# mLSTM attention with a bilinear layer on one core: a gate table for the first time chunk, later gates moved, a longer search for the order, and tiles on multiples of 128 bytes

## The chip, the core and the metric

The kernel runs on one core of one Trainium2 chip. The metric is the device time in microseconds (us) of one execution, the median of several runs. The engines of the core are named as in the profile: PE (TensorE, the matmuls), PEld (the loading of its weights), DVE (VectorE), ACT (ScalarE), POOL (GpSimd) and SP (SyncE, which here issues every DMA).

## The reference

Gated linear attention over 4 batches, 8 heads, 768 time steps and 40 columns per head, and behind it a bilinear layer on all 3072 tokens:

```python
for t in range(S):                                   # S = 768, for each of 4 x 8 heads
    m_new = max(f[t] + m, i[t])
    f_stab = exp(f[t] + m - m_new);  i_stab = exp(i[t] - m_new);  m = m_new
    C = f_stab * C + i_stab * outer(v[t], k[t]);  n = f_stab * n + i_stab * k[t]
    y[t] = sigmoid(o[t]) * (C @ q[t]) / max(abs(n . q[t]), 1)
x = y as (3072 tokens, 8 * 40 = 320)
out = ((x @ w_a) * (x @ w_b)) @ w_out                # 320 -> 1536 -> 320
```

The three weights are float64; the other inputs are float32.

## The kernel before

**Attention.** Time is cut into 6 chunks c of 128 steps, so there are 24 pairs n = (c, b) of a chunk and a batch. Inside a pair the recurrence becomes matrix products under a mask, with tables of gate terms; between chunks of one batch the state `cst` is carried. `first_gates` makes the running maximum and sums of the gates for chunk 0, `later_gates` for chunks 1 to 5: scans and sums on DVE over tiles of 32 rows (32 = batch times head), which lie in `qks2` and `qks3`. From them come `g_dram` (sent out by a DMA and read back, spread over 128 rows, as `gbc`), and `gtab`, a table with time on the partitions, made by transposes on PE (`ptg`) and an Exp on ACT. The pairs below NS = 2 are done ahead of everything else; the pairs 2 to 5 (`early_chunk`, with `begin_a`, `begin_b`, ...) use plain float32 matmuls, the later ones bf16 pieces.

**The bilinear layer.** Its token blocks have 2, 2, 3, 3, 3, 3, 3, 2 and 3 pairs of 128 tokens (`sizes`). For each block and each of 12 slices `ff` of 128 hidden columns, `up` makes two sums `pu` of 8 float32r matmuls each (x and the weights are each split into a high and a low part, `xh`, `xl` and the two planes of `w`), DVE multiplies them to `g`, this is split into `gh` and `gl`, and `down`, two slices later, adds 3 matmuls per token tile to `pd`. So a block makes 12 * (16 + 3 * tiles) such matmuls.

**Conversion of the weights.** The weights arrive as 32 slices `raw0` to `raw31` of float64 bits. Each passes through `high` (ACT), `low` (DVE for the first five, ACT after), `join` (DVE, the operation on `cw`), `lead_part` (a copy into `w` by ACT or DVE) and `low_part` (a DVE subtraction into `w`). Block 0 uses the slices as they get ready; from block 1 on all are there.

**What sets the order.** The program is first recorded as nodes. A list scheduler, `Plan.run`, then places them with a cost for each (`Plan.cost`), and `settle` repeats this `TURNS` times with disturbed ranks, replays each order under four sets of disturbed costs, and keeps the one with the least mean end. Copies may go to ACT or DVE (`copier`), some sums to DVE or POOL (`adder`): the scheduler chooses. Each engine then runs its instructions in the order written, and waits where its next one isn't ready. While PE would wait in the first part, the scheduler lays in small matmuls `warm` (bf16, 256 columns, result unused); this ends as soon as another tile of the same PSUM buffer `pd2` is used, which `ptg` is.

The attention beside the blocks is one generator, which starts so:

```python
def rest():
    gates = later_gates()
    for _ in range(2):
        next(gates)
        yield
    yield from begin_a(NS)
    yield from begin_e(NS)
    yield from gates
```

All recorded instructions have the profile's line L522, the `warm` matmuls L515 (L528 and L521 in the changed file).

Of the kernel before, what the change touches and what calls it, by code (L numbers as in the profile page):

```python
# [18 lines left out]
AF = mybir.ActivationFunctionType  # L19
ALU = mybir.AluOpType  # L20
PSUM = bass.MemoryType.PSUM
TURNS = 40
TRIALS = 4
SPREAD = 0.3
LANES = 8
# [80 lines left out]


class Node:
    __slots__ = ("i", "eng", "alts", "calls", "by", "prev", "next", "table", "acc", "wide", "use", "pair", "least")

    def __init__(self, i, alts):
        self.i, self.alts, self.eng = i, alts, alts[0]
        self.calls, self.prev, self.next, self.acc = [], {}, [], []
        self.by = {e: [0.0, 0.0, 0.0, False] for e in alts}
        self.table, self.wide, self.use = None, True, 0.0


class Plan:
# [8 lines left out]

    def __init__(self, nc):
        self.nc, self.nodes, self.filler, self.bank = nc, [], None, None
        self.pair, self.least = False, 0.0  # L130
# [50 lines left out]
    def cost(self, node, by, eng, op, out, refs, args, kw):  # L181


        cols = int(np.prod(out.shape[1:]))
        size = [x.size if isinstance(x, View) else mybir.dt.size(x.dtype) for x in refs]
        psum = [isinstance(x, View) and x.root.ring[0] == "psum" for x in refs]
        if eng == "PE":
            if op == "transpose":
                occ = 0.109
            else:  # L190
                f32 = [str(x.dtype) if not isinstance(x, View) else x.kind() for x in refs[1:3]]
                if size[1] == 2:
                    occ = cols / 2400 + 0.005 if cols > 64 else 0.026
                elif "float32r" in f32[0]:
                    occ = cols / 2400 + 0.0135
                else:
                    occ = 0.224 if cols <= 128 else cols / 600 + 0.01
                    if refs[1].shape[0] <= 64:
                        occ = 0.135
                    elif out.shape[0] <= 64:  # L200
                        occ = 0.06
            by[0] += occ
            by[1] = 0.17
            plain = size[1] == 4 and op == "matmul" and "float32r" not in f32[0]
            node.use += cols * refs[1].shape[0] * (1 + plain) / 128.0 * out.shape[0] / 128.0
        elif eng == "ACT":
            func = str(args[2]) if op == "activation" else "Copy"
            node.table = "S" if "Sigmoid" in func else "E" if "Exp" in func else None
            bias = hasattr(kw.get("bias"), "shape")
            by[0] = 0.04 + cols * (0.00084 if any(psum) else 0.00094) + (0.13 if bias else 0.0)  # L210
            by[0] += 0.05 if "Prelu" in func or "scale" in kw else 0.0
            by[1] = 0.11
        elif eng == "DVE":
            rate = 960.0
            one = op in ("tensor_copy", "copy", "tensor_scalar", "memset", "tensor_scalar_max") and not any(psum)
            if one:
                rate = 1920.0 if max(size) == 4 else 3840.0
            if op == "tensor_tensor_scan":
                rate = 480.0
            by[0] = 0.065 + cols / rate  # L220
            by[1] = 0.085
            by[3] = (one or len(refs) > 2) and not any(psum)
        elif eng == "POOL":
            by[0] = 0.03 + cols * 0.00205
            if op == "affine_select":
                by[0] = 0.05 + cols * 0.001
            elif op == "memset":
                by[0] = 0.05 + cols * 0.0008
            by[1] = 0.06
            by[3] = op != "memset"  # L230
        elif op == "dma_start_transpose":
            by[0], by[1] = 1.3, 1.6
        else:
            n = int(np.prod(out.shape)) * size[0]
            node.wide = out.shape[-1] * size[0] > 512
            by[0], by[1] = 0.47 if node.wide else 0.6, 1.7
            by[2] = n / (305e3 if node.wide else 160e3)

    def link(self):
        last, rings = {}, {}  # L240
        for node in self.nodes:
            for key, box, write in node.acc:
                if isinstance(key, Root):
                    if key.first is None:
                        key.first = node
                        rings.setdefault(key.ring, []).append(key)
                    else:
                        self.edge(key.first, node, order=True)
                    key.users.append(node)
                mine = last.setdefault(key, [])  # L250
                for k, b, w in mine:
                    if (w or write) and k is not node and all(p < y and x < q for (p, q), (x, y) in zip(b, box)):
                        self.edge(k, node)
                if write:
                    mine[:] = [
                        z for z in mine
                        if not all(x <= p and q <= y for (p, q), (x, y) in zip(z[1], box))
                    ]
                mine.append((node, box, write))
        for ring in rings.values():  # L260
            for a, b in zip(ring, ring[1:]):
                self.edge(a.first, b.first, order=True)
            for a, b in zip(ring, ring[ring[0].ring[2]:]):
                for k in a.users:
                    self.edge(k, b.first)
# [18 lines left out]
    def run(self, rank, forward=True, fixed=None, odds=None):  # L284
# [18 lines left out]
        order, count, filling = [], 0, False  # L303

        def put(x, r):
            if forward:
# [51 lines left out]
        while count < len(nodes):  # L358
# [56 lines left out]
            if e == "PE" and forward:  # L415
# [6 lines left out]
                while filling and fixed is None:  # L422
# [130 lines left out]
def kernel(  # L553
# [77 lines left out]
    nc.gpsimd.affine_select(  # L631
        mask, mask, pattern=[[1, P]], compare_op=ALU.is_ge, fill=-1e30, base=0, channel_multiplier=-1
    )
    one = wpool.tile([BH, 1], F32, name="one")
    nc.gpsimd.memset(one, 1.0)

    plan.least = 2.1
# [96 lines left out]
    def first_gates():  # L734
# [11 lines left out]
        for j in range(3):  # L746
            x = gb3[j]
            (nc.scalar.copy if j < 2 else nc.vector.tensor_copy)(stk[j * BH:(j + 1) * BH], top(x))
            if j < 2:
                nc.vector.tensor_tensor(gb3[j + 1], x, top(x), op=ALU.subtract)  # L750

    def later_gates():
        f, i, m = (x[:, P:] for x in (gf, gi, gm))
        G = tab[0:BH]
# [3 lines left out]
        nc.vector.tensor_tensor(f, f, m, op=ALU.subtract)  # L758
        nc.vector.tensor_tensor(i, i, m, op=ALU.subtract)
        yield  # L760
        nc.scalar.copy(G[:, 0], gb3[0][:, 0])
        nc.scalar.copy(tab[BH:2 * BH, 0], gb3[0][:, 1])
        for c in range(1, NC):
            nc.vector.tensor_tensor_scan(
                G[:, c], one.broadcast_to([BH, P]), gf[:, c * P:(c + 1) * P], 0.0,
# [1 line left out]
            )  # L767
            if c == 3:
                yield
        nc.sync.dma_start(g_dram.rearrange("c g t -> g c t"), G)  # L770
        ends = wpool.tile([BH, NC - 2, BH // 2], F32, name="ends")
        nc.gpsimd.tensor_tensor(
            ends, G[:, 1:NC - 1, P - 1:].broadcast_to([BH, NC - 2, BH // 2]),
# [4 lines left out]
        nc.vector.tensor_tensor(tab[BH:2 * BH, 1:], beta, G[:, 1:], op=ALU.subtract)  # L778
        yield
        nc.vector.tensor_tensor(  # L780
            tab[2 * BH:], tab[BH:2 * BH], G[:, :, P - 1:P].broadcast_to([BH, NC, P]), op=ALU.add
        )
        yield
        for half in range(2):
            pt = ps_dn.tile([P, 512], F32, tag="pd2", name="ptg")
            n3 = NC // 2
            for c in range(n3):
                nc.tensor.transpose(
                    pt[:, c * 3 * BH:(c + 1) * 3 * BH], tab[:, half * n3 + c, :],
                    ident[0:3 * BH, 0:3 * BH],  # L790
                )
            n0, n1 = (BH, n3 * 3 * BH) if half == 0 else (0, (n3 * 3 - 1) * BH)
            nc.vector.tensor_copy(
                gtab[:, half * (n3 * 3 - 1) * BH:][:, 0:n1 - n0], pt[:, n0:n1]
            )
            yield
        x = gtab[:, BH:].rearrange("p (c g) -> p c g", g=3 * BH)[:, :, 0:2 * BH]
        nc.scalar.activation(x, x, AF.Exp)
        pt = ps_dn.tile([P, 512], F32, tag="pd2", name="pdec")[:, 0:(NC - 2) * BH // 2]
        nc.tensor.matmul(  # L800
# [3 lines left out]
        nc.scalar.activation(dec.rearrange("p c x -> p (c x)"), pt, AF.Exp)  # L804
        yield

    def g_col(c, b, x):
        return gtab[:, (3 * c + x) * BH + b * H:][:, 0:H]

    def beta_col(c, b):  # L810
        return g_col(c, b, 0)
# [1 line left out]
    def w_col(c, b):  # L813
        return g_col(c, b, 1)

    def a_col(c, b):
        return g_col(c - 1, b, 2)


    def weight_stages():  # L820
# [778 lines left out]
```

## Time and profile before

| | |
|---|---|
| median of 3 runs | 534.51 us (534.0 to 534.91) |
| profiled execution | 534.12 us, its span 532.3 us, mean granted TensorE clock 0.994 |
| DVE busy | 411.4 us (77%), 919 instructions |
| ACT busy | 236.3 us (44%), 568 instructions |
| POOL busy | 147.9 us (28%), 194 instructions |

A span runs from the first to the last instruction of the profile; 1.8 us of the execution lie around it. In rows of the timeline stand the start, the busy time, the engine, line and operation, the tiles as output <- inputs with their shape, how many like instructions the row joins, and in brackets how long the engine had been idle before it and what ended that. Rows of groups give the count, then total busy us and mean ns of one. PE's matmuls are pipelined, so what one costs is read from start to start.

### The profile page before, as it was taken

How to read it: one execution, taken by the hardware profiler on the slowest of the kernel's cores; microseconds unless marked ns; L12 is line 12 of the kernel's file. 1: busy time of each engine (PE TensorE's matmuls, PEld its weight loads, DVE VectorE, ACT ScalarE, POOL GpSimd, SP SyncE). 2: the span in 40 equal slices, each digit the busy share in tenths (PEclk: the TensorE clock that was granted, in tenths of full speed). 3: DMA queues.
4: the chain of work that ended last, by engine and by line, in shares of the span. 5: the costliest groups of instructions: out<-in, count | busy, mean ns of one | idle time of the engine just before them, and what ended most of it. 6: DMA issues, size and time to landing. Idle time of an engine off the chain costs nothing.

```text
span 532.3 us, 12505 instructions
## 1 busy us (share of the span) xinstructions
PE 523.2 (98%) x4862; PEld 497.1 (93%) x4862; DVE 411.4 (77%) x919; ACT 236.3 (44%) x568; POOL 147.9 (28%) x194
## 2 busy tenths in 40 slices
PE   8889999999999999999999999999999999999997
PEld 6679999999999999999999999999999999999997
DVE  5999999799979859888599776888489848843332
ACT  5759997543456142346243344543215515212111
POOL 2015134414326505534223423526050301000000
PEclk9899999999999999999999999999999999999999
DMA  9998866978696864886755766765537427000001
GB/s 172 305 245 182 238 167 135 137 148 165 117 188 129 148 146 104 155 158 104 169 105 97 158 119 157 155 99 114 130 73 140 93 41 156 2 1 25 2 1 37
DMA packets 198679, 66.77 MB, mean 125 GB/s; under 512 B 184252, under 2 KB 191900, under 8 KB 198620
## 3 DMA queue, kind: packets, MB, share of 16 engines
q1 hardware_dynamic: 198620, 65.98, 59.6%
q8 instruction: 38, 0.62, 0.5%
q14 instruction: 21, 0.17, 0.1%
HBM read 41.11 MB, written 5.97 MB: 88 GB/s over the span
## 4 chain that ended last, share of the span: by engine, by line
PE 81%; DVE 7%; issue 3%; DMA 2%; ACT 2%; SPq 1%; POOL 0%; ACTq 0%; DVEq 0%; POOLq 0%
PE pu L522 46%; PE pd L522 22%; PE pV L522 4%; PE pS L522 3%; PE pU L522 2%; DVE qks L522 2%; DVE w L522 2%; PE pI L522 2%; SPq L522 1%; PE pX L522 1%; DMA qk<-in_k_dram 1%; DVE cw L522 1%; DMA gbc<-g_dram 1%; DMA c_dram<-cb 1%; DVE osig L522 1%
## 5 line engine op out<-in xcount | busy, mean ns | idle before, releaser
L522 PE MATMUL pu<-xh,w 128*128 128x384 f32 (+1 forms) x1080 | 277.2, 325 | 0.1
L522 PE MATMUL pu<-xl,w 128*128 128x384 f32 (+1 forms) x648 | 203.9, 323 | 0.9 <-DVE xl L522 0.9
L522 PEld LDWEIGHTS pu<-xh,w 128*128 128x128 f32 x1080 | 190.0, 189 | 1.7 <-ACT xh L522 0.6
L522 PE MATMUL pd<-w,gh 128*128 128x320 f32 x576 | 135.1, 315 | 0.3 <-ACT gh L522 0.2
L522 PEld LDWEIGHTS pu<-xl,w 128*128 128x128 f32 x648 | 121.1, 189 | 1.4 <-DVE xl L522 1.2
L522 PEld LDWEIGHTS pd<-w,gh 128*128 128x128 f32 x576 | 97.0, 188 | 1.0 <-ACT gh L522 0.7
L522 DVE TENSOR_TENSOR g<-pu,g 128x384 f32<-128x384 f32 (+1 forms) x108 | 54.6, 506 | 53.4 <-PE pu L522 50.2
L522 ACT COPY g<-pu 128x384 f32<-128x384 f32 (+1 forms) x99 | 43.7, 442 | 113.8 <-PE pu L522 112.6
L522 PE MATMUL pd<-w,gl 128*128 128x320 f32 x288 | 86.6, 310 | 0.1
L522 ACT ACTIVATE gbc<-gbc,gtab 128x128 f32<-128x128 f32 x160 | 52.7, 394 | 3.3 <-POOL gbc L522 3.3
L522 PEld LDWEIGHTS pd<-w,gl 128*128 128x128 f32 x288 | 53.4, 188 | 0.3 <-DVE gl L522 0.3
L522 POOL TENSOR_TENSOR gl<-g,gh 128x384 fp32r<-128x384 f32 (+1 forms) x24 | 26.4, 1102 | 81.4 <-ACT gh L522 46.0
L522 DVE TENSOR_TENSOR gl<-g,gh 128x384 fp32r<-128x384 f32 (+1 forms) x84 | 46.4, 553 | 2.1 <-DVE gh L522 0.5
L522 ACT CAST gh<-g 128x384 fp32r<-128x384 f32 (+1 forms) x44 | 20.5, 465 | 39.9 <-DVE g L522 39.8
L522 DVE TENSOR_TENSOR gbc<-pS,gbc 128x512 f32<-128x512 f32 x48 | 32.6, 681 | 4.7 <-ACT gbc L522 3.7
L522 POOL TENSOR_TENSOR vr<-va 128x336 f32<-128x336 f32 x18 | 14.0, 775 | 79.0 <-PE pV L522 71.1
L522 PE MATMUL pV<-va,gbc 128*128 128x42 bf16 (+1 forms) x240 | 34.5, 221 | 0.0
L522 POOL TENSOR_TENSOR vw<-va,gtab 128x336 f32<-128x336 f32 x20 | 16.2, 808 | 64.9 <-PE pU L522 58.1
L522 PEld LDWEIGHTS <-T 120*128 120x128 bf16 x576 | 25.4, 97 | 7.6 <-issue 5.1
L522 DVE TENSOR_TENSOR gbc<-gbc,pb 128x512 f32<-128x512 f32 x36 | 29.4, 817 | 0.4 <-ACT pb L522 0.3
L522 DVE TENSOR_TENSOR pb<-gbc 128x512 bf16<-128x512 f32 x36 | 29.0, 806 | 0.3
L522 POOL TENSOR_SCALAR_AFFINE_SELECT gbc<-gbc 128x1024 f32<-128x1024 f32 x20 | 25.0, 1248 | 11.7 <-DMA gbc<-g_dram 11.7
(109 smaller groups left out, 768.7 us busy)
## 6 DMA issues: line engine op xcount, KB each, us to landing
gbc<-g_dram SPq DMA_DIRECT2D x20, 512.0 KB
qk<-in_q_dram SPq DMA_DIRECT2D x24, 160.0 KB
qk<-in_k_dram SPq DMA_DIRECT2D x24, 160.0 KB
va<-in_v_dram SPq DMA_DIRECT2D x24, 160.0 KB
osig<-in_o_gate_dram SPq DMA_DIRECT2D x24, 160.0 KB
raw<-in_moe_w_out_dram SPq DMA_DIRECT2D x12, 320.0 KB
out_dram<-o SPq DMA_DIRECT2D x24, 160.0 KB
raw<-in_moe_w_a_dram SPq DMA_DIRECT2D x8, 384.0 KB
```

The lines of the kernel that those rows point to most:

```text
L522: f(*[real(x) for x in args], **{k: real(x) for k, x in kw.items()})
```

## The change

- **Order and costs.** `TURNS` goes from 40 to 150. The scheduler's cost of a float32r matmul becomes 0.452 ns per column and 1.5 ns, and it adds 0.1 us where PE goes between matmuls over all 128 rows, over at most 64 rows, and into at most 64 rows (`mode`).
- **A table for chunk 0.** `first_weights` makes the one column of `gtab` that chunk 0 needs from the first gates alone: a DVE sum, a PE transpose, an ACT Exp. An ordering edge puts this Exp ahead of the two first Sigmoids.
- **Later gates.** `later_gates` is recorded at pair NS + 1 and not ahead of pair NS; it makes chunks 1 to 5 alone, so that two ACT copies and one of six `ptg` transposes go, `g_dram` is written for five chunks, the two copies into `gtab` may go to ACT, and one small Exp is added.
- **Addresses.** The tile `one` is 32 float32 wide and not 1. The tiles behind it in the pool, `gtab`, `dec`, `raw`/`w`, `vr`, `T`, `gbc`, `osig`, `xh`, `xl`, `g`, `gh`, `gl`, `cw` among them, move from 32 bytes past a multiple of 128 to a multiple of 128; `qk`, `va`, `qks` and `cst` stay.

```diff
-TURNS = 40
+TURNS = 150
...
                 elif "float32r" in f32[0]:
-                    occ = cols / 2400 + 0.0135
+                    occ = cols * 0.000452 + 0.0015
...
+            node.mode = 1 if refs[1].shape[0] <= 64 else 2 if out.shape[0] <= 64 else 0
...
+        for a, b in self.orders:
+            self.edge(a, b, order=True)
...
+                if x.mode != mode:
+                    t += 0.1
+                    mode = x.mode
...
-    one = wpool.tile([BH, 1], F32, name="one")
+    one = wpool.tile([BH, 32], F32, name="one")[:, 0:1]
...
         nc.scalar.activation(x, x, AF.Sigmoid)
+        if c == 0 and b < NS:
+            plan.orders += [(e, plan.nodes[-1]) for e in exps]
...
+    def first_weights():
+        w0 = gf[:, 0:P]
+        nc.vector.tensor_scalar(w0, gb3[0][:, 1], gb3[0][:, 0, P - 1:], None, op0=ALU.add)
+        pw = ps_up.tile([P, NTB], F32, tag="pu", name="pw")[:, 0:BH]
+        nc.tensor.transpose(pw, w0, ident[0:BH, 0:BH])
+        nc.scalar.activation(gtab[:, BH:2 * BH], pw, AF.Exp)
+        exps.append(plan.nodes[-1])
...
-        nc.scalar.copy(G[:, 0], gb3[0][:, 0])
-        nc.scalar.copy(tab[BH:2 * BH, 0], gb3[0][:, 1])
...
-        nc.sync.dma_start(g_dram.rearrange("c g t -> g c t"), G)
+        nc.sync.dma_start(g_dram[1:].rearrange("c g t -> g c t"), G[:, 1:])
...
         nc.vector.tensor_tensor(
-            tab[2 * BH:], tab[BH:2 * BH], G[:, :, P - 1:P].broadcast_to([BH, NC, P]), op=ALU.add
+            tab[2 * BH:, 1:], tab[BH:2 * BH, 1:], G[:, 1:, P - 1:P].broadcast_to([BH, NC - 1, P]),
+            op=ALU.add,
         )
...
-            nc.vector.tensor_copy(
-                gtab[:, half * (n3 * 3 - 1) * BH:][:, 0:n1 - n0], pt[:, n0:n1]
-            )
+            n1 = (len(cs) * 3 - half) * BH
+            nc.copier.copy(gtab[:, (3 * cs[0] - 1) * BH:][:, 0:n1], pt[:, 0:n1])
             yield
-        x = gtab[:, BH:].rearrange("p (c g) -> p c g", g=3 * BH)[:, :, 0:2 * BH]
+        nc.scalar.activation(a_col(1, 0, B), a_col(1, 0, B), AF.Exp)
+        x = gtab[:, 4 * BH:].rearrange("p (c g) -> p c g", g=3 * BH)[:, :, 0:2 * BH]
...
         for n in range(NS, NCH):
+            if n == NS + 1:
+                yield from later_gates()
+                load_g(NE)
             yield from (early_chunk if n < NF32 else late_chunk)(n)
...
     run(E[1], 2)
+    first_weights()
...
     def rest():
-        gates = later_gates()
-        for _ in range(2):
-            next(gates)
-            yield
         yield from begin_a(NS)
         yield from begin_e(NS)
-        yield from gates
```

What this does to the instructions: PE has 12 `warm` matmuls of 256 columns and not 52; DVE 909 instructions and not 921, ACT 576 for 570, POOL 206 for 199. Three places of the order show it. In the names the last number counts buffers; `xl0`, `xh0` are the x of block 0, `pX1` the transposed output of pair 1, from which its second half comes.

SP at its start, before. The first two rows fetch the gates of chunk 0:

```order
L522 DMA qks2_88<-in_f_gate_dram 32x128
L522 DMA qks2_88<-in_i_gate_dram 32x128
L522 DMA qk0_80<-in_q_dram 128x8x40
L522 DMA qk0_80<-in_k_dram 128x8x40
L522 DMA qk1_81<-in_q_dram 128x8x40
```

And after:

```order
L528 DMA qks2_88<-in_f_gate_dram 32x128
L528 DMA qk0_80<-in_q_dram 128x8x40
L528 DMA qks2_88<-in_i_gate_dram 32x128
L528 DMA qk0_80<-in_k_dram 128x8x40
L528 DMA raw0_157<-in_moe_w_a_dram 128x384
```

The input gate is now asked for behind q of pair 0.

DVE where `xl0` gets its second half, before (the operations on `qks2` and `qks3` are the later gates):

```order
L522 TENSOR_TENSOR osig0_234<-pV1_346,osig0_234 128x320
L522 SCALAR_TENSOR_TENSOR qks2_88<-qks2_88 32x640
L522 SCALAR_TENSOR_TENSOR cw_390<-qks1_87,cw_390 128x384
L522 TENSOR_TENSOR qks2_88<-qks2_88 32x640
L522 TENSOR_TENSOR w4_359<-cw_338,w4_359 64x384
L522 TENSOR_TENSOR qks2_88<-qks2_88 32x640 x2
L522 SCALAR_TENSOR_TENSOR qks3_89<-one_102,qks2_88 32x128 x5
L522 TENSOR_TENSOR w1_387<-cw_363,w1_387 128x384
L522 TENSOR_TENSOR qks3_89<-qks2_88,qks3_89 32x640
L522 TENSOR_TENSOR xl0_398<-pX1_414,xh0_392 128x3x128
L522 TENSOR_TENSOR qks3_89<-qks3_89 32x768
```

And after:

```order
L528 TENSOR_TENSOR osig0_260<-pV1_364,osig0_260 128x320
L528 SCALAR_TENSOR_TENSOR cw_406<-qks1_87,cw_406 128x384
L528 TENSOR_TENSOR xl0_439<-pX0_400,xh0_410 128x3x128
L528 SCALAR_TENSOR_TENSOR cw_425<-qks1_87,cw_425 128x320
L528 TENSOR_TENSOR w3_441<-cw_406,w3_441 128x384
L528 SCALAR_TENSOR_TENSOR cw_445<-qks0_86,cw_445 128x320
L528 TENSOR_TENSOR xl0_439<-pX1_435,xh0_410 128x3x128
L528 SCALAR_TENSOR_TENSOR qks2_88<-qks2_88 32x640
L528 SCALAR_TENSOR_TENSOR cw_451<-qks1_87,cw_451 128x320
L528 TENSOR_TENSOR w5_468<-cw_425,w5_468 128x320
L528 TENSOR_TENSOR qks2_88<-qks2_88 32x640
```

The gates, which stood ahead of `xl0`'s second half, now begin behind it, between the conversions of later slices.

PE at the end of block 0, where the last slice `w31` is first used, before:

```order
L522 MATMUL pd0_0_663<-w31_1377,gh0_11_1432 128x320 x2
L522 MATMUL pd0_0_663<-w31_1377,gl0_11_1440 128x320
L522 MATMUL pd0_1_668<-w30_1355,gh0_10_1414 128x320 x2
L522 MATMUL pd0_1_668<-w30_1355,gl0_10_1425 128x320
L522 MATMUL pd0_1_668<-w31_1377,gh0_11_1432 128x320 x2
L522 MATMUL pd0_1_668<-w31_1377,gl0_11_1440 128x320
L522 MATMUL pu1_0_0_1470<-xh1_943,w0_310 128x256
```

And after (`pT5` are transposes of q and k of pair 5, `pV4` a product of pair 4):

```order
L528 MATMUL pd0_0_666<-w31_1325,gh0_11_1366 128x320 x2
L528 MATMUL pd0_0_666<-w31_1325,gl0_11_1378 128x320
L528 MATMUL pT5_0_1391<-ident_75,qk2_82 128x128 x4
L528 MATMUL pT5_1_1399<-ident_75,qk2_82 128x128 x4
L528 MATMUL pd0_1_668<-w30_1318,gh0_10_1338 128x320 x2
L528 MATMUL pd0_1_668<-w30_1318,gl0_10_1346 128x320
L528 MATMUL pV4_1416<-va1_84,gbc4_747 128x42 x8
L528 MATMUL pd0_1_668<-w31_1325,gh0_11_1366 128x320 x2
L528 MATMUL pd0_1_668<-w31_1325,gl0_11_1378 128x320
L528 MATMUL pu1_0_0_1439<-xh1_1009,w0_254 128x256
```

`pT5` and `pV4`, which stood 75 rows or more ahead of `w31`'s first use, now stand behind it.

More of the change, by code (lines that the diff above doesn't have):

```diff
@@ L108 @@
 class Node:
-    __slots__ = ("i", "eng", "alts", "calls", "by", "prev", "next", "table", "acc", "wide", "use", "pair", "least")
+    __slots__ = ("i", "eng", "alts", "calls", "by", "prev", "next", "table", "acc", "wide", "use", "pair", "least", "mode")
     def __init__(self, i, alts):
@@ L114, in __init__ @@
         self.by = {e: [0.0, 0.0, 0.0, False] for e in alts}
-        self.table, self.wide, self.use = None, True, 0.0
+        self.table, self.wide, self.use, self.mode = None, True, 0.0, 0
 class Plan:
@@ L129, in __init__ @@
         self.nc, self.nodes, self.filler, self.bank = nc, [], None, None
-        self.pair, self.least = False, 0.0
+        self.pair, self.least, self.orders = False, 0.0, []
         for name in self.ENGINES:
@@ L302, in run @@
         other = {"DVE": "POOL", "POOL": "DVE"}
-        order, count, filling = [], 0, False
+        order, count, filling, mode = [], 0, False, 0
         def put(x, r):
@@ L750, in first_gates @@
                 nc.vector.tensor_tensor(gb3[j + 1], x, top(x), op=ALU.subtract)
+    exps = []
+    def first_weights():
[5 more added lines that the diff above has]
+        exps.append(plan.nodes[-1])
     def later_gates():
@@ L786, in later_gates @@
             n3 = NC // 2
-            for c in range(n3):
+            cs = range(max(half * n3, 1), (half + 1) * n3)
+            for x, c in enumerate(cs):
                 nc.tensor.transpose(
-                    pt[:, c * 3 * BH:(c + 1) * 3 * BH], tab[:, half * n3 + c, :],
-                    ident[0:3 * BH, 0:3 * BH],
-                )
-            n0, n1 = (BH, n3 * 3 * BH) if half == 0 else (0, (n3 * 3 - 1) * BH)
-            nc.vector.tensor_copy(
-                gtab[:, half * (n3 * 3 - 1) * BH:][:, 0:n1 - n0], pt[:, n0:n1]
-            )
+                    pt[:, x * 3 * BH:(x + 1) * 3 * BH], tab[:, c, :], ident[0:3 * BH, 0:3 * BH]
+                )
+            n1 = (len(cs) * 3 - half) * BH
+            nc.copier.copy(gtab[:, (3 * cs[0] - 1) * BH:][:, 0:n1], pt[:, 0:n1])
             yield
-        x = gtab[:, BH:].rearrange("p (c g) -> p c g", g=3 * BH)[:, :, 0:2 * BH]
+        nc.scalar.activation(a_col(1, 0, B), a_col(1, 0, B), AF.Exp)
+        x = gtab[:, 4 * BH:].rearrange("p (c g) -> p c g", g=3 * BH)[:, :, 0:2 * BH]
         nc.scalar.activation(x, x, AF.Exp)
@@ L805, in later_gates, with g_col @@
         yield
-    def g_col(c, b, x):
-        return gtab[:, (3 * c + x) * BH + b * H:][:, 0:H]
+    def g_col(c, b, x, nb=1):
+        return gtab[:, (3 * c + x) * BH + b * H:][:, 0:nb * H]
     def beta_col(c, b):
@@ L814, in w_col, with a_col @@
         return g_col(c, b, 1)
-    def a_col(c, b):
-        return g_col(c - 1, b, 2)
+    def a_col(c, b, nb=1):
+        return g_col(c - 1, b, 2, nb)
     def weight_stages():
@@ L1538, in rest @@
         squash(0, NS, B - NS)
-        load_g(NE)
         yield from attention()
```

## The prediction

> **What bounds the kernel now.** The page first: which engine is busy, and in which stretch it isn't.
>
> ```profile
> span 532.3 us, 12505 instructions
> PE 523.2 (98%) x4862; PEld 497.1 (93%) x4862; DVE 411.4 (77%) x919; ACT 236.3 (44%) x568; POOL 147.9 (28%) x194
> ```
>
> PE is the bound of the whole, but an average of 98% says nothing of the first 90 us, where the change lies. So next the busy time by windows (start and end, length, then the busy us of PE, PEld, DVE, ACT and POOL, the granted clock, the DMA share and GB/s):
>
> ```profile
> 10.24:30.70 20.46, 17.26 (x137) 13.83 (x135) 19.85 (x45) 13.25 (x27) 0.49 (x3) 0.83 1.05 269
> 30.70:57.00 26.30, 25.81 (x283) 24.07 (x284) 24.96 (x57) 23.36 (x51) 9.20 (x12) 1.00 0.92 232
> 57.00:88.40 31.40, 31.07 (x263) 29.34 (x262) 30.61 (x71) 28.62 (x78) 11.78 (x17) 1.00 0.67 161
> ```
>
> From 10.24 to 88.40 DVE is idle for 0.61 + 1.34 + 0.79 = 2.7 us of 78.2. It is as full as PE there, and PE's busy time in the first window holds work whose result nobody uses. The timeline tells who waits for whom, on both engines:
>
> ```profile
> 23.36 0.56 DVE L522 SCALAR_TENSOR_TENSOR cw<-qks,cw 128x384 uint32<-128x384 uint32 x1
> 24.09 5.24 PE L515 MATMUL warm<-idle 128*128 128x256 bf16 x28
> 30.08 0.56 DVE L522 TENSOR_TENSOR xl<-pX,xh 128x384 fp32r<-128x384 f32 x1
> 30.69 0.39 PE L522 MATMUL pu<-xl,w 128*128 128x256 f32 x1 [0.93 <-DVE xl L522]
> 85.24 0.47 DVE L522 TENSOR_TENSOR w<-cw,w 128x320 fp32r<-128x320 f32 x1
> 87.13 0.46 PE L522 MATMUL pd<-w,gh 128*128 128x320 f32 x2
> ```
>
> PE fills 5.24 us with 28 unused matmuls and then waits for the second half of `xl0`, ready at 30.08 + 0.56; the sums of block 0 start at 30.69. They then keep step with the conversion: the low part of the last slice, w31, ends at 85.24 + 0.47 = 85.71, and PE first uses it at 87.13. Behind that point no weight is awaited any more, and PE alone sets the rest, 532.3 - 87.13 = 445.2 us. So two numbers give the time: when w31 is there, and how much PE has still to do then.
>
> **The earlier start.** DVE's groups from 10 to 86 us (total us, mean ns):
>
> ```profile
> L522 DVE TENSOR_TENSOR w<-cw,w 128x320 fp32r<-128x320 f32 x12 | 7.0, 599 | 0.0
> L522 DVE COPY T<-pT 128x512 f32<-128x512 f32 x4 | 2.7, 681 | 0.3 <-PE pT L522 0.3
> L522 DVE CAST w<-cw 128x320 fp32r<-128x320 f32 x8 | 2.4, 317 | 0.0
> L522 DVE TENSOR_TENSOR qks<-qks 32x640 f32<-32x640 f32 x3 | 2.4, 814 | 0.1
> L522 DVE TENSOR_TENSOR gl<-g,gh 128x256 fp32r<-128x256 f32 x4 | 2.3, 564 | 0.0
> L522 DVE TENSOR_TENSOR_SCAN qks<-one,qks 32x128 f32<-32x128 f32 x5 | 1.7, 391 | 0.0
> L522 DVE TENSOR_TENSOR_SCAN qks<-qks 32x640 f32<-32x640 f32 x1 | 1.5, 1542 | 0.0
> L522 DVE TENSOR_TENSOR qks<-qks 32x768 f32<-32x768 f32 x1 | 0.9, 950 | 0.0
> L522 DVE COPY gtab<-ptg 128x256 f32<-128x256 f32 x2 | 0.8, 418 | 0.0
> L522 DVE TENSOR_TENSOR qks<-qks,qks 32x640 f32<-32x640 f32 x1 | 0.8, 815 | 0.0
> L522 DVE COPY g<-pu 128x256 f32<-128x256 f32 x1 | 0.4, 420 | 0.0
> ```
>
> The later gates are the rows on `qks` of 32 partitions: 2.4 + 1.7 + 1.5 + 0.9 + 0.8 = 7.3 us, of which all but the 32x768 row, 6.4 us, stand ahead of that second half. The change puts them behind it. In their place come two joins of `cw` at the 0.56 of the row at 23.36, so 1.1 us. A cost comes at the very beginning:
>
> ```profile
> 1.20 0.41 SPq L522 DMA_DIRECT2D qks<-in_i_gate_dram  x1
> 1.66 0.42 SPq L522 DMA_DIRECT2D qk<-in_q_dram  x1
> ...
> 3.10 0.44 DVE L522 TENSOR_TENSOR_SCAN qks<-qks 32x128 f32<-32x128 f32 x1 [0.56 <-DMA qks<-in_i_gate_dram]
> ```
>
> The first scan waits for the input gate, whose DMA now goes out one place later: 1.66 - 1.20 = 0.46 us at least. What q ahead of it holds it up on the wire can't be seen; I take 0.5 for DVE's full stretch, between 0.46 and about 1. Together: sums of block 0 start 6.4 - 1.1 - 0.5 = 4.8 us earlier, near 25.9. The 40 `warm` matmuls that go were the filling of that wait and cost nothing.
>
> **What the conversion makes of it.** The gates aren't gone; they stand behind `xl0` but still ahead of w31 on an engine with 2.7 us to spare. So w31 moves only by what leaves DVE before it. Counted in the order up to w31: 5 casts of `w` (1.6 us at 317 ns), 3 copies of `T` (2.0), the 2 copies of `gtab` (0.8, now ACT's) and one `xl` (0.56) go; the 32x768 row becomes 32x640 (0.1). That is 5.1 us. More there are 3 copies of `g` (1.3 at 420), 2 subtractions `gl` (1.1 at 564), one product `g` (0.4, as the copy of that shape), 2 casts of 64x384 (0.7, by columns from the 317 of 320), one update of the state and the new small sum (an estimate of 0.5 for both): 4.0 us; and two short ones go, again an estimate of 0.5. Net 1.6 us less. Of the 2.7 us idle a quarter may go, 0.6: fewer waits for `xl0` and `ptg`, but the same for ACT. Then w31 ends at 85.71 + 0.5 - 1.6 - 0.6 = 84.0. Bounds: 82 if all idle time goes, 85.7 if nothing is gained. PE, which now starts 4.8 us earlier with the same work per slice, will stand waiting there, so it uses w31 at about 84.1, 3.0 us sooner than the 87.13 of before.
>
> **What PE has still to do behind that point.** More than before, by two terms. Three rows of like order to those moved, and a piece of the steady part:
>
> ```profile
> 58.61 0.60 PE L522 MATMUL pT<-ident,qk 128*128 128x128 f32 x4
> 59.05 1.90 PE L522 MATMUL pV<-va,gbc 128*128 128x42 f32 x16
> 60.77 0.36 PE L522 MATMUL pu<-xh,w 128*128 128x256 f32 x1
> ...
> 240.70 0.34 PE L522 MATMUL pu<-xl,w 128*128 128x384 f32 x1
> 240.88 0.33 PE L522 MATMUL pu<-xh,w 128*128 128x384 f32 x1
> 241.05 0.62 PE L522 MATMUL pS<-T,T 120*128 120x128 bf16 x8
> 241.48 0.42 PE L522 MATMUL pu<-xh,w 128*128 128x384 f32 x1
> 241.74 0.33 PE L522 MATMUL pu<-xl,w 128*128 128x384 f32 x1
> ```
>
> The two groups `pT5` and the group `pV4` now stand behind w31's first use. From start to start one `pT` takes 59.05 - 58.61 = 0.44 and `pV` 60.77 - 59.05 = 1.72: 2 * 0.44 + 1.72 = 2.6 us. In the old order they lay where PE kept step with DVE anyway.
>
> The second term: a float32r matmul of 384 columns takes 240.88 - 240.70 = 0.18 from start to start, but 241.74 - 241.48 = 0.26 where it comes right behind a bf16 group. So each change from bf16 to float32r costs 0.08 to 0.09 us. Counted behind w31, the old order has 115 of them and the new one 141: 26 * 0.085 = 2.2 us. The scheduler's new 0.1 us knows changes in rows, not this one. (Lower bound 0, if the surplus sits at other places than this row shows; upper bound 26 * 0.1.)
>
> Sum: -3.0 + 2.6 + 2.2 = +1.8 us on the profiled execution's 534.12, which stands 0.4 below the median; on the median 534.51 + 1.8 = 536.3. Its own range, by w31 between 82 and 85.7 and the alternations between 0.5 and 2.6 us: 534.51 - 87.13 + 82 + 2.6 + 0.5 = 532.5 at the lowest, 538.3 at the highest; I use 534 to 538.3, as both ends together are unlikely.
>
> **Edits with no price.** The Exp of chunk 0 and the copies of `gtab` go to ACT, which in 10.24 to 88.40 is busy 65.2 of 78.2 us and has the room; the write of `g_dram`, a sixth smaller, has no reader before pair 4, tens of us later. Were ACT full, the two copies of `gtab` would bring back their 0.8 us. The search itself runs ahead of the execution.
>
> **The addresses** might cost or bring something everywhere, and the trace has all the tiles concerned on one offset. What it shows is the price per column:
>
> ```profile
> 61.09 0.40 PE L522 MATMUL pu<-xh,w 128*128 128x256 f32 x2
> 61.33 0.28 PE L522 MATMUL pu<-xl,w 128*128 128x256 f32 x1
> ```
>
> 256 columns take (61.33 - 61.09) / 2 = 0.12 and 384 take (241.05 - 240.70) / 2 = 0.175: 0.43 ns per column and a rest of 0.120 - 0.110 = 10 ns. If that rest were due to operands 32 bytes off, 12 * (16 * 9 + 3 * 24) = 2592 matmuls would give back 26 us; if it is the start of each matmul, nothing. I take nothing: an offset should cost all along the columns, while this rest is paid once for each matmul, as its start would be. [...]
>
> **The rivals.**
>
> Faster: the earlier start is kept. It decides at the time of w31: with +4.8 behind it, the kernel is faster by 1.07 us (0.2%, about what a measurement of this kernel can tell from no change) if w31 is used before 87.13 - 4.8 - 1.1 = 81.2, or correspondingly later if alternations are cheaper. For it: the 599 ns mean of the `w` subtraction against 470 in the row at 85.24, so 12 * 0.13 = 1.5 us of that group is stretched by something beside it, and more in other groups; less of that and less idle time could bring w31 to 79 to 80. Against it: nothing in the change takes POOL's or ACT's work away. Its time, with w31 at 79.5: 534.51 - 7.6 + 4.8 = 531.7; with the whole 4.8 us kept and PE never waiting, 529.7.
>
> Slower by a new wait: DVE gets later. POOL has 206 instructions and not 199; up to w31 the products on `osig` go from 3 on POOL to 8.
>
> ```profile
> L522 POOL TENSOR_TENSOR vw<-va,gtab 128x336 f32<-128x336 f32 x20 | 16.2, 808 | 64.9 <-PE pU L522 58.1
> ```
>
> A product of about that size takes POOL 0.8 us. If each of the five more holds DVE up for half to all of it, w31 is 2 to 4 us later, at 86 to 88, and the time 538.3 to 540.3, say 539. [...]
>
> The addresses matter: 534.51 + 1.8 - 26 is 510; DVE's 411.4 us of work would allow it. Say 508 to 522.
>
> The clock: the window 10.24:30.70 has 0.83. If PE, without its filling, fell to half clock once more for some 4 us, the loss of 2 us would lie where it waits for DVE; only two or more such stretches after 60 us would show, giving 540 or more.
>
> **How the numbers follow.** The forecast (536.3) gets 0.47: the DVE count is the best supported part, its idle time the weakest. The kept start gets 0.29, since 3 us on a stretch of 75 decide it. The POOL wait gets 0.15, the addresses 0.06, the clock 0.03. The forecast's own part splits into 0.03 faster, 0.13 within 0.2% and 0.31 slower; the kept start into 0.28 and 0.01. Faster: 0.03 + 0.28 + 0.06 = 0.37; same 0.14; slower 0.31 + 0.15 + 0.03 = 0.49. The range from 529.7 to 540.3 leaves out the addresses, the clock and the ends of the others, about 0.15.
>
> **What would show it.** Right: no later gates ahead of `xl0`'s second half, sums of block 0 starting near 26, no run of 28 `warm` matmuls, PE gaps spread over 30 to 84 with DVE `w` or `cw` as releaser, w31's low part ending near 84, and behind its first use some 450 us of PE without gaps. Wrong: w31 ending before 81 or after 86; matmuls of 256 columns at 0.11 from start to start; the `pu` behind a bf16 group no later than others; clock under 1.0 after 30 us.

## The result, and the profile after

The changed kernel takes 537.65 us (median of 6 runs, 536.94 to 538.44); the kernel before, run beside it, 534.82. The ratio is 1.0052, 95% interval 1.0036 to 1.0067: slower by 2.8 us. The profiled execution took 538.44 us, the longest of the six.

The head of its page, the same two lines as before:

```profile
span 536.3 us, 12428 instructions
PE 526.5 (98%) x4822; PEld 496.9 (93%) x4822; DVE 409.9 (76%) x907; ACT 237.6 (44%) x574; POOL 149.9 (28%) x201
```

PE is busy 3.3 us longer with 40 matmuls fewer. The windows (length, then busy us of PE, PEld, DVE, ACT, POOL, granted clock, DMA share, GB/s):

```profile
10.24:30.70 20.46, 18.31 (x162) 16.49 (x160) 17.32 (x39) 15.98 (x37) 1.56 (x2) 0.67 1.10 260
30.70:57.00 26.30, 24.89 (x228) 22.47 (x227) 25.84 (x58) 24.22 (x52) 7.60 (x13) 1.00 0.94 246
57.00:88.40 31.40, 30.46 (x268) 27.88 (x265) 30.93 (x74) 28.24 (x78) 8.96 (x15) 1.00 0.70 156
```

DVE is still full from 30.7 on, 56.8 of 57.7 us, but in the first window it now stands idle for 3.1 us where it was 0.6. And the clock of that window fell from 0.83 to 0.67. The timeline at the two points from which the prediction worked:

```profile
4.62 0.42 DVE L528 TENSOR_TENSOR_SCAN qks<-qks 32x128 f32<-32x128 f32 x1 [2.09 <-DMA qks<-in_i_gate_dram]
...
26.20 0.55 DVE L528 TENSOR_TENSOR xl<-pX,xh 128x384 fp32r<-128x384 f32 x1
26.63 1.08 PE L528 MATMUL pE<-cx 96*128 96x128 bf16 x8
27.46 0.56 PE L528 MATMUL pu<-xl,w 128*128 128x256 f32 x1
...
82.96 1.03 DVE L528 TENSOR_TENSOR w<-cw,w 128x320 fp32r<-128x320 f32 x1
83.77 0.69 PE L528 MATMUL pd<-w,gh 128*128 128x320 f32 x2
84.39 0.50 DVE L528 TENSOR_TENSOR gl<-g,gh 128x256 fp32r<-128x256 f32 x1
84.94 0.42 PE L528 MATMUL pd<-w,gl 128*128 128x320 f32 x1 [0.48 <-DMA osig<-in_o_gate_dram]
85.19 1.04 PE L528 MATMUL pT<-ident,qk 128*128 128x128 f32 x8
86.70 1.98 PE L528 MATMUL pV<-va,gbc 128*128 128x42 f32 x16
```

The sums of block 0, counted from the first use of the second half of `xl0`, start at 27.46 instead of 30.69, and w31 is used at 83.77 instead of 87.13. So 3.2 us of earlier start are there, and arrive at w31 in full. What is left behind that point has grown from 445.2 to 536.3 - 83.77 = 452.5 us, by 7.4. The 4.0 us between the two spans are -3.4 + 7.4. (The wait at 84.94 is put down to the DMA of an output gate, but that matmul reads `gl`, and DVE's `gl` in the row above it ends at 84.89; in e9, which has the same order, the same wait is put down to `gl`.)

Where the 7.4 us lie, counted from start to start over all matmuls behind w31's first use: with each at the median of its kind and neighbours in the kernel before, the new order has 5.4 us more work, and 2.0 us more are waits beyond these medians (4.8 and 2.6 where the kinds are grouped in another way). The first part is the 26 further steps from bf16 to float32r (2.2 us), three further ones from plain float32, and the groups `pT5` and `pV4` in the rows above. Of the waits PE's own list behind 85 us shows, for the changed kernel, only

```profile
PE pu L528 <- DVE g L528: 0.5, 1, 0.5
PE pd L528 <- DMA osig<-in_o_gate_dram: 0.5, 1, 0.5
PE pX L528 <- DVE gbc L528: 0.2, 1, 0.2
```

(us in all, times, longest), where the kernel before has 0.3 and 0.2.

### The profile page after: what moved, and what is told of

Same layout as the page of the kernel before. It is cut to its first block, busy times and chain, and to the rows that moved or that the text cites. A ratio compares the mean times of both kernels' runs of the same rounds, so it can differ in the third digit from the quotient of the medians.

```text
span 536.3 us, 12428 instructions
## 1 busy us (share of the span) xinstructions
PE 526.5 (98%) x4822; PEld 496.9 (93%) x4822; DVE 409.9 (76%) x907; ACT 237.6 (44%) x574; POOL 149.9 (28%) x201
## 4 chain that ended last, share of the span: by engine, by line
PE 90%; DVE 6%; ACT 1%; issue 1%; DMA 1%; SPq 0%; ACTq 0%; DVEq 0%
PE pu L528 49%; PE pd L528 23%; PE pV L528 6%; PE pS L528 4%; PE pU L528 2%; PE pI L528 2%; PE pX L528 2%; DVE qks L528 2%; DVE w L528 1%; PE warm L528 1%; PE pT L528 1%; DVE g L528 1%; DMA osig<-in_o_gate_dram 1%; DVE cw L528 1%; PE pE L528 1%
## 5 line engine op out<-in xcount | busy, mean ns | idle before, releaser
L528 PE MATMUL pu<-xh,w 128*128 128x384 f32 (+1 forms) x1080 | 282.2, 328 | 2.8 <-DVE g L528 1.4
L528 PE MATMUL pd<-w,gh 128*128 128x320 f32 x576 | 137.5, 316 | 0.0
L528 ACT COPY g<-pu 128x384 f32<-128x384 f32 (+1 forms) x95 | 42.4, 447 | 124.4 <-PE pu L528 122.6
L528 PE MATMUL pd<-w,gl 128*128 128x320 f32 x288 | 87.9, 311 | 0.5 <-DMA osig<-in_o_gate_dram 0.5
L528 POOL TENSOR_TENSOR gl<-g,gh 128x384 fp32r<-128x384 f32 (+1 forms) x26 | 26.7, 1027 | 52.4 <-ACT gh L528 40.6
L528 PE MATMUL pV<-va,gbc 128*128 128x42 bf16 (+1 forms) x240 | 37.1, 231 | 0.1
L528 ACT CAST gh<-g 128x384 fp32r<-128x384 f32 (+1 forms) x47 | 21.9, 466 | 34.0 <-DVE g L528 33.5
L528 DVE TENSOR_TENSOR gbc<-gbc,pb 128x512 f32<-128x512 f32 x36 | 31.2, 866 | 0.4 <-ACT pb L528 0.3
L528 POOL TENSOR_SCALAR_AFFINE_SELECT gbc<-gbc 128x1024 f32<-128x1024 f32 x20 | 26.7, 1334 | 13.0 <-DMA gbc<-g_dram 10.9
```

Source lines behind the costliest of these rows:

```text
L528: f(*[real(x) for x in args], **{k: real(x) for k, x in kw.items()})
```

## The experiments

In all of them two readings of the profile carry the verdict: when w31 is first used, and how long the span goes on behind it. "Steps" are the changes to float32r from another kind of matmul behind w31, counted in the order. Each row's times are of its profiled execution, but for the median.

| run | median us | sums start | w31 used | rest of the span | steps |
|---|---|---|---|---|---|
| before | 534.51 | 30.69 | 87.13 | 445.2 | 127 |
| changed | 537.65 | 27.46 | 83.77 | 452.5 | 156 |
| e1 before, new addresses | 534.29 | 30.65 | 86.98 | 445.0 | 127 |
| e2 changed, old addresses | 537.14 | 26.77 | 82.56 | 452.6 | 156 |
| e3 changed, a step priced at 0.3 | 542.37 | 26.58 | 85.26 | 453.9 | 103 |
| e4 changed, gates early | 535.64 | 29.33 | 89.48 | 444.6 | 131 |
| e5 changed, filled | 539.58 | 29.38 | 85.62 | 452.8 | 156 |
| e6 changed, 100 small apart | 549.78 | 26.87 | 83.18 | 464.6 | 256 |
| e7 changed, 100 small beside | 540.37 | 26.81 | 83.13 | 455.5 | 156 |
| e8 changed, old costs | 535.97 | 26.32 | 85.01 | 448.8 | 144 |
| e9 changed, more DVE | 547.10 | 26.67 | 92.19 | 452.7 | 156 |
| e10 changed, real prices | 532.80 | 25.62 | 85.20 | 445.1 | 109 |
| e11 gates early, real prices | 536.14 | 29.94 | 87.09 | 447.9 | 120 |
| e12 changed, price alone | 541.87 | 28.64 | 85.95 | 453.6 | 138 |

**e1 and e2: the addresses alone.**

```diff
-    one = wpool.tile([BH, 1], F32, name="one")             # e1; e2 is the reverse in the changed kernel
+    one = wpool.tile([BH, 32], F32, name="one")[:, 0:1]
```

> The kernel before with one edit, the tile one 32 wide: the order of all instructions stays, the tiles behind it move to multiples of 128 bytes. My theory (the addresses bring and cost nothing): within 0.2% of the kernel before, 533.7 to 535.9, and float32r matmuls of 256 and 384 columns still 0.120 and 0.175 us from start to start. Rival (the addresses matter): 508 to 522 if they help, near 537 if they are what made the changed kernel slower.

> The changed kernel with the tile one 1 wide again, so with the old addresses and the new order. My theory: as the changed kernel, 536.5 to 538.5. Rival (the 2.8 us of loss come from the addresses): 534.8.

Measured: e1 534.29 us, ratio to before 0.9995 (0.9981 to 1.0009); e2 537.14, ratio 1.0039 (1.0025 to 1.0052), whose interval overlaps that of the changed kernel. In e1, at the place that the prediction read:

```profile
240.56 0.34 PE L522 MATMUL pu<-xl,w 128*128 128x384 f32 x1
240.74 0.33 PE L522 MATMUL pu<-xh,w 128*128 128x384 f32 x1
240.92 0.62 PE L522 MATMUL pS<-T,T 120*128 120x128 bf16 x8
241.35 0.42 PE L522 MATMUL pu<-xh,w 128*128 128x384 f32 x1
241.60 0.33 PE L522 MATMUL pu<-xl,w 128*128 128x384 f32 x1
```

(240.92 - 240.56) / 2 = 0.18 us from start to start, and 0.25 behind the bf16 group: as with the old addresses. They bring and cost nothing that shows.

**e6 and e7: what a step costs.** Both add the same 100 matmuls (bf16, 64 columns, zeros added to an open sum `pd`) to the changed kernel's order, in one case apart, between float32r matmuls, in the other behind a bf16 matmul.

```diff
+                self.nc.tensor.matmul(
+                    self.side(extra[id(node)]), self.spare, self.spare[:, 0:64], start=False, stop=False
+                )
```

> The changed kernel with 100 bf16 matmuls more (64 columns, zeros added to an open sum) in blocks 2 to 7, each alone between float32r matmuls, so 100 more steps from bf16 to float32r. My theory (a step costs 0.084 us on PE, as read from start to start): the same 100 beside bf16 groups, plus 8.4 us, so about 549 to 551. Rival (what follows a bf16 group is late for another reason): as with the 100 beside.

> The changed kernel with the same 100 bf16 matmuls of 64 columns, each behind a matmul of a bf16 group, so no further step from bf16 to float32r. Both theories: 0.03 to 0.06 us for each, so 3 to 6 us more than the changed kernel, 540.5 to 543.5.

Measured: 549.78 and 540.37 us, each with two runs. Beside, one adds 0.03 us; apart, another 0.094. The rest of the span differs by 9.1 us. First a matmul apart, of e6, then one beside, of e7:

```profile
172.14 0.34 PE L545 MATMUL pu<-xh,w 128*128 128x384 f32 x1
172.32 0.20 PE L547 MATMUL pd<-spare 128*128 128x64 bf16 x1
172.36 0.42 PE L545 MATMUL pu<-xh,w 128*128 128x384 f32 x1
172.62 0.34 PE L545 MATMUL pu<-xl,w 128*128 128x384 f32 x1
```

```profile
239.17 0.18 PE L545 MATMUL pV<-vr,pb 128*128 128x42 bf16 x1
239.19 0.19 PE L547 MATMUL pd<-spare 128*128 128x64 bf16 x1
239.22 0.42 PE L545 MATMUL pu<-xh,w 128*128 128x384 f32 x1
239.47 0.33 PE L545 MATMUL pu<-xl,w 128*128 128x384 f32 x1
```

In both, the float32r matmul behind a bf16 one holds PE for 0.25 to 0.26 us and not 0.175; in e7 that step was there before. So the price is the step's, as the prediction had it, and it isn't hidden.

**e9: is it DVE that sets w31?**

```diff
+            if node.eng == "DVE" and name in SLICES and node.calls[0][0] == "tensor_tensor":   # w8 to w21
+                for _ in range(2):
+                    self.nc.vector.tensor_tensor(self.spare, self.spare, self.spare, op=ALU.add)
```

> The changed kernel with 32 useless DVE additions of 128x128, two behind each low part of the slices w8 to w21, so between 30 and 70 us, about 0.2 us each (an estimate by columns from the 0.48 us of 320), 6 to 7.5 us in all. The order is kept. My theory (DVE's work sets when w31 comes, PE waits along): w31 comes 6 us later or more, and the time is 543 to 545. Rival (after the start of the sums PE's own work sets it, the way from there to w31 having been 56 us before and after): at most 2 us more, 537.5 to 539.5.

Measured: 547.10 us (two runs), ratio 1.0229, about 2 us above what I expected. The additions are dearer than estimated: 26 of them took 0.27 to 0.29 us, and six, each beside a POOL instruction, 0.38 to 1.17. The group's row, and one pair beside POOL:

```profile
L533 DVE TENSOR_TENSOR spare<-spare 128x128 f32<-128x128 f32 x32 | 11.4, 357 | 0.7
57.51 1.41 POOL L529 TENSOR_SCALAR_AFFINE_SELECT gbc<-gbc 128x1024 f32<-128x1024 f32 x1
57.89 1.93 DVE L533 TENSOR_TENSOR spare<-spare 128x128 f32<-128x128 f32 x2
```

PE has the room to wait for them (two windows):

```profile
30.70:57.00 26.30, 22.43 (x190) 20.43 (x189) 25.72 (x69) 20.49 (x44) 4.78 (x11) 0.94 0.97 257
57.00:88.40 31.40, 25.95 (x228) 22.85 (x228) 30.91 (x74) 26.02 (x67) 8.85 (x14) 1.00 0.48 110
```

DVE is as full as ever, PE falls from 55.4 to 48.4 us busy in the two windows, and the way from the first sums to w31 goes from 56.3 to 65.5 us, 9.2 more. From the first sums to the end of w31's low part DVE is busy for 64.2 of 65.8 us, where the changed kernel has 55.4 of 56.5: 8.8 us more (the 11.4 of the group overlap their neighbours). The rest of the span stays at 452.7. More DVE work makes w31 later, nearly one for one; PE's rival is out. What less DVE work would bring isn't shown by this run. Nor is it quite pure: in the first of these windows PE's clock fell once more, to a mean of 0.94.

**e4 and e8: parts of the change undone.** e4 records the later gates at their old place; e8 gives the scheduler its old costs.

```diff
     def attention():                                       # e4
         for n in range(NS, NCH):
-            if n == NS + 1:
-                yield from later_gates()
-                load_g(NE)
...
     def rest():
+        gates = later_gates()
+        for _ in range(2):
+            next(gates)
+            yield
         yield from begin_a(NS)
         yield from begin_e(NS)
+        yield from gates
...
+        load_g(NE)
...
-                    occ = cols * 0.000452 + 0.0015         # e8
+                    occ = cols / 2400 + 0.0135
...
-                if x.mode != mode:
-                    t += 0.1
-                    mode = x.mode
```

> The changed kernel with the later gates recorded at their old place, ahead of pair 2, all else as changed. Its order has 131 steps to float32r behind the first use of w31 (127 in the kernel before, 156 in the changed one), pT5 and pV4 ahead of it, and 39 warm matmuls of 256 columns. My theory (what PE has left behind w31 decides, and w31 comes with the DVE work ahead of it, which is within 1 us of the kernel before): 534 to 536.5, although the earlier start is given up. Rival (the first table, the new costs or the addresses make the loss): 537 or more.

> The changed kernel with the scheduler's costs of before (float32r by columns at 2400 per us and 0.0135, no price for a change of rows); first table, later gates, 150 turns and addresses as changed. Its order has 144 steps to float32r behind the first use of w31 (156 changed, 127 before), pT5 and pV4 partly ahead of it, and DVE about 1.8 us less work ahead of w31 by the mean of each form. My theory (w31's time and what PE has left behind it add up): w31 near 82.5, behind it 2.3 us less than changed, so 534 to 536. Rival (the new costs have no part in the loss): 537 or more.

Measured: e4 535.64 us, ratio 1.0009 (0.9997 to 1.0021), e8 535.97, ratio 1.0018 (1.0004 to 1.0031). Both times fell where I expected them, but not by their terms, so in part by luck. In e4 the rest behind w31 is short again (444.6), while w31 came at 89.48, 2.4 us later than in the kernel before. I had counted 0.7 us more DVE work, by the mean of each form; from the first scan to the end of w31's low part DVE was in fact busy for 77.0 us and idle for 7.9, against 75.8 and 6.8 in the kernel before. In e8 w31 came at 85.01, not 82.5, and the rest fell by 3.7, not 2.3. There DVE, for which I had counted 1.8 us less than changed, was busy for 75.8 us, the changed kernel's for 74.7; and PE's clock stood at 0.50 once more from 46.5 to 49.9, amid the conversion. The mean work of the forms ahead of w31 is too rough to tell orders apart by 2 us.

**e5: the clock.** In windows of 3.4 us the changed kernel shows when the clock fell:

```profile
14.54:17.95 3.41, 3.41 (x39) 3.16 (x37) 3.33 (x9) 3.36 (x8) 1.11 (x2) 0.84 1.11 279
17.95:21.36 3.41, 3.14 (x15) 2.99 (x14) 3.03 (x9) 1.22 (x3) 0.46 (x1) 0.50 1.03 357
21.36:24.78 3.42, 2.53 (x22) 1.91 (x22) 3.36 (x10) 2.74 (x9) 0.00 (x0) 0.50 1.19 239
24.78:28.19 3.41, 2.42 (x15) 2.06 (x14) 3.38 (x6) 3.41 (x10) 0.00 (x0) 0.50 0.91 239
28.19:31.60 3.41, 3.41 (x30) 3.36 (x29) 3.14 (x6) 2.66 (x7) 0.00 (x0) 0.66 1.18 238
```

e5 lays unused matmuls into that stretch (the 40 behind another matmul write into free columns of the bank of `pU`):

```diff
+AHEAD_OF = {'pU0': 4}
+BEHIND = {'pV1': 12, 'pX0': 10, 'pX1': 10, 'pu0_0_0': 8}
...
```

> The changed kernel, its order kept, with 4 more unused matmuls of 256 columns and 40 of 128 columns laid around pV1, pX0, pX1 and the first pu, where PE stands at half clock from about 17 to 30 us. My theory (DVE's conversion decides when w31 comes; the slow clock only adds what it holds DVE up): the clock is granted in full for one or two windows of 3.4 us more, w31 is first used at 81 to 82.5, the time is 535.5 to 537. Rival (the slow clock ate the earlier start, and the change would be faster without it): w31 near 79 and 532 to 534. Rival (the unused matmuls lie in the way): slower than 538.

Measured: 539.58 us, so the third of these came true, and my 535.5 to 537 is a miss. The clock of the window from 10.24 to 30.70 is 0.83 again, but the fillers lie in the way, and the sums start later:

```profile
22.64 0.87 PE L534 MATMUL pX<-ident,osig 128*128 128x128 f32 x3 [1.99 <-DVE den L534]
29.38 0.36 PE L534 MATMUL pu<-xl,w 128*128 128x256 f32 x1
```

27.46 became 29.38, and w31 moved from 83.77 to 85.62: the start's 1.9 us come out at the end, in the same order. What a full clock without anything in the way would bring was not separated. The changed kernel's six runs give a hint: at a mean clock of 0.987 they took 538.44, 537.62 and 538.16 us, at 0.990 537.69, 536.94 and 537.37, on the mean 0.7 less.

**e3, e12, e10, e11: a scheduler that knows the price.** e3 charges 0.3 us for a step in place of the 0.1 for a change of rows; e12 charges 0.085; e10 does that with the old cost of a float32r matmul; e11 is e10 with the gates early.

```diff
-                if x.mode != mode:
-                    t += 0.1
-                    mode = x.mode
+                if x.turn and not turning:      # x.turn: a float32r matmul
+                    t += 0.085                  # e3: 0.3
+                turning = x.turn
...
-                    occ = cols * 0.000452 + 0.0015     # e10 and e11 alone
+                    occ = cols / 2400 + 0.0135
```

> The changed kernel, its scheduler charging 0.3 us for each step from another kind of matmul to a float32r one, in place of the 0.1 us for a change of rows. Counted in its order behind the first use of w31, 103 such steps instead of 156 (68 from bf16 instead of 121). My theory (each costs 0.084 us and nothing hides it): 537.65 - 53 * 0.084 = 533.2, between 531.5 and 535. Rival (the loss comes from the slow clock up to 30 us, or from elsewhere in block 0, which this leaves as it is, with 13 warm matmuls of 256 columns): 537 or more.

> The changed kernel with one edit of the two of e10: 0.085 us for each step to float32r in place of the 0.1 us for a change of rows, the new cost of a float32r matmul kept. 138 steps behind the first use of w31 (109 in e10, 144 in e8, 156 changed). My theory (the rest behind w31 goes with the steps): w31 at 84 to 85.5, behind it 1.5 to 2.5 us less than changed, 534.5 to 536.5, between e8 and e10. Rival (the price alone does what e10 did): 532.5 to 533.5.

> The changed kernel, its scheduler with the old cost of a float32r matmul and, in place of the 0.1 us for a change of rows, 0.085 us for each step to float32r, as the traces show it. Its order has 109 such steps behind the first use of w31 (156 changed, 127 before), at the early start of the changed kernel. My theory: w31 near 84.5, behind it some 4 us less than changed if no new waits come: 533 to 535.5, a little faster than before. Rival (fewer steps are bought with waits for g and x, as at a price of 0.3): 537 or more.

> As the run before, but with the later gates recorded at their old place ahead of pair 2. 120 steps to float32r behind the first use of w31, 63 warm matmuls of 256 columns. My theory: sums of block 0 start about as before (29 to 31), w31 at 86.5 to 89, and behind it about 1 us less than before: 533 to 536.5. Rival (waits instead of steps): 537 or more.

Measured: e3 542.37 us, e12 541.87 (ratio 1.0115, 1.0083 to 1.0147), e10 532.80 (ratio 0.9961, 0.9945 to 0.9976), e11 536.14 (1.0011, 0.9993 to 1.003). e3 and e12 are misses. e10 is a little faster than I expected; e11 is within its range, but its rest behind w31 is 2.7 us longer than before and not 1 us shorter. e3 did get rid of 53 steps, and counted at medians its work behind w31 is 5.4 us less than changed; it lost more in waits, and behind one of them at a clock of 0.50. Rows of its timeline, two windows, and PE's list of waits behind 85 us:

```profile
98.72 0.47 PE L531 MATMUL pd<-w,gh 128*128 128x320 f32 x2
102.01 0.64 PE L531 MATMUL pd<-w,gl 128*128 128x320 f32 x1 [2.82 <-DVE gl L531]
```

```profile
98.45:101.86 3.41, 0.74 (x6) 0.47 (x4) 1.85 (x2) 0.72 (x3) 3.09 (x5) 1.00 0.95 182
101.86:105.27 3.41, 3.26 (x14) 3.17 (x15) 3.34 (x11) 1.89 (x5) 0.71 (x1) 0.50 0.91 165
```

```profile
PE pd L531 <- DVE gl L531: 2.8, 1, 2.8
PE pd L531 <- DVE gh L531: 2.5, 3, 1.3
PE pX L531 <- DVE gbc L531: 0.3, 1, 0.3
PE pU L531 <- DVE xl L531: 0.2, 1, 0.2
```

In the window behind the long wait the clock is 0.50, and the matmuls there take 1.6 us longer than at their medians. e12, where I expected 534.5 to 536.5, has waits of the same sort, at full clock by its numbers (0.71 from 10.24 to 30.70 and 0.97 from there to 57.00 account for the run's mean of 0.987):

```profile
PE pd L531 <- DVE gh L531: 2.6, 2, 1.3
PE pX L531 <- DVE gbc L531: 0.6, 2, 0.5
```

e10 has none: PE's list of waits behind 85 us is empty. It starts early, has 109 steps and no waits, and is the fastest of all kernels here, its span 530.3 us:

```profile
25.62 0.58 PE L531 MATMUL pu<-xl,w 128*128 128x256 f32 x1
85.20 0.46 PE L531 MATMUL pd<-w,gh 128*128 128x320 f32 x2
```

The rest behind w31 is 445.1, with `pT5` and `pV4` still in it. Its order asks for the input gate ahead of q again, and its first scan starts at 3.04 as in the kernel before. Since e12 differs from e10 only in the cost of a float32r matmul by 1 to 3 ns, and lies 9 us higher, the gain of e10 can't be put down to the price alone: the search finds quite different orders for small differences, and its costs don't show it which of them will wait.

## Why the prediction was right

Forecast was 536.3 us, slower, in a range of 529.7 to 540.3; 537.65 was measured. The mechanism holds: an earlier start, w31 set by DVE (e9), and more left for PE behind w31 (e4, e6, e7). Its terms:

- **First scan 0.5 us later**: it was 4.62 - 3.10 = 1.5, above the upper end of about 1. The DMA of the input gate went out 0.46 later, at 1.66; the other 1.0 passed between its issue and the scan. All runs with that gate behind q have the scan at 4.5 to 4.8, and all with it ahead, e3, e4, e10 and e11 too, at 2.9 to 3.1. Mis-sized by 1.0.
- **Sums 4.8 us earlier, near 25.9**: 3.2 us, at 27.46. `xl0` was there at 26.75, 3.9 us sooner than before; the late scan may account for what is missing there, but no run has it alone. Then PE still had a `pE` group to do, 0.83 us for 8 matmuls (from 26.63, at a clock of 0.50); 24 of them took 1.47 us at 1.00 (from 11.96, in the same run), so the clock made some 0.3 us of this, an estimate. A part also changes from one execution to the next: e2, e6, e7 and e9, with the same order up to there, start the sums at 26.7 to 26.9, and the first three use w31 at 82.6 to 83.2. In these four the clock fell later (in 14.54 to 17.95 it was 0.94 in e7 and 1.00 in the others, against 0.84).
- **w31's low part at 84.0**: 82.96 + 1.03 = 83.99. The value is right in part by luck, since three sizes were off and cancel. From the first scan to the end of w31's low part DVE was busy for 75.8 us before and 74.7 after, 1.1 less where I had 1.6; idle for 6.8 and 4.7, 2.1 less where I had 0.6; and the scan came 1.5 later, not 0.5: 85.7 + 1.5 - 1.1 - 2.1 = 84.0. The idle time went where I hadn't looked, ahead of 10.24. The windows from the first scan on, before and after:

```profile
3.10:10.24 7.14, 6.91 (x65) 4.91 (x64) 3.09 (x11) 3.81 (x9) 1.23 (x6) 1.00 1.22 209
4.62:10.24 5.62, 5.49 (x51) 4.57 (x49) 4.95 (x15) 2.54 (x5) 0.00 (x0) 1.00 1.16 226
```

That is 4.1 us idle before and 0.7 after. From 10.24 to 88.4, where I let a quarter of DVE's idle time go, it grew instead, from 2.7 to 4.1 us. And PE doesn't stand waiting in a body ahead of w31: from 30.7 to 88.4 it is busy for 55.4 of 57.7 us, and its list of waits from 24 to 84 has 0.4 us for `w`, beside 1.0 for `xh` and 0.9 for `g`. The way from the first sums to w31 is 56.3 us, as the 56.4 before: nothing of the earlier start was lost in block 0.

- **Behind w31 4.8 us more**: 5.4 more in work. The price of a step, 0.085, is 0.084 in the trace and 0.094 in e6 against e7. From bf16 there are 95 such steps before and 121 after, not 115 and 141; the difference of 26 is the same. The moved groups take 0.80 and 1.81 us from start to start, the 2.6 that I took.
- **Missing: waits behind w31**, 2.0 us. I had looked for waits only ahead of that point; the list of waits shows `g` and `gbc` from DVE, and the rows at 84.39 and 84.94 `gl`. With the 0.6 of further work, less 0.4 at w31, they make the 2.2 us between my +1.8 and the +4.0 of the spans; on the medians the forecast was 1.4 low.
- **The rivals.** The addresses are out (e1 at a ratio of 0.9995, e2 at 1.0039). I took nothing for them because an offset should cost all along the columns; that was an assumption, which no run shows; measured are 0.18 us from start to start for 384 columns, in e1 as in the kernel before. The POOL rival assumed that each further product holds DVE up for half to all of its time. Its w31 at 86 to 88 didn't come, though the stretching that it builds on is there: of the 36 `w` subtractions on DVE up to w31's, 8 before and 7 after took 0.65 to 1.37 us, each of them beside a POOL instruction, and the others 0.44 to 0.56. What they were stretched by sums to 3.5 us before and 2.8 after, so it didn't grow. w31's own subtraction, 1.03 us at 82.96, is one of them:

```profile
82.85 0.79 POOL L528 TENSOR_TENSOR r<-qk,qks 128x320 f32<-128x320 f32 x1 [1.51 <-ACT qks L528]
```

The kept start came true in its first half, w31 3.4 us sooner, and was outweighed. The clock rival was given too little: the clock did fall, for 13.7 us up to 30.5 where it had been 6.8, and in the place where I said it would be covered it held up PE's `pE` group and with it the first sums. It fell inside the window from 14.54, to a mean of 0.84 there and 0.50 in the next, with PE busy, by the profile, for all of the first one's 3.41 us, mostly in matmuls of 42 columns.

## What to carry to other kernels

Where a second engine feeds the first up to some point, take the time at that point and the work left behind it as two numbers, and read both from the trace: an earlier start counts only as far as it isn't paid back behind (here -3.4 and +7.4 us). What a matmul took here depended on its neighbours (0.26 us for 384 float32r columns behind a bf16 matmul, and 0.175 among their kind); count the changes of kind in an order before and after. A list scheduler that is given a better price may still come out slower (e12, by 4 us against the changed kernel), since its orders differ in waits that no price in it knows: run several orders, choose by the measured time, and read the profile's list of waits for the reason.

## What the runs showed that I had not expected

PE was busy throughout a window, by the profile, and its clock fell all the same: 3.41 of 3.41 us busy, clock 0.84 and then 0.50, while the kernel before, with another order and 62 `warm` matmuls in all where the changed one has 22, kept the full clock to 21.37, and e5 brought 0.67 back to 0.83. And beside POOL some DVE instructions took up to about four times as long: six additions of e9 took 0.38 to 1.17 us in place of 0.27 to 0.29, and the 15 `w` subtractions over 0.6 us, before and after, all ran beside POOL. That POOL is the reason was not tested by a run of its own, and not every DVE instruction beside POOL was slowed: of the 57 subtractions of 0.44 to 0.56 us, 11 ran for over half of their time beside one of POOL.
